# Two-level down product in three more chunks, and weight sums made by negation on ScalarE and adding loads from DRAM

## The chip, the cores and the metric

The kernel runs on one core of a Trainium2 chip, in fp32 throughout. The metric is the device time of one execution in microseconds (us); the median of several executions is compared. The engines are TensorE (PE, matmuls; PEld is its weight load), VectorE (DVE), ScalarE (ACT), GpSimd (POOL), and SyncE (SP), which issues most of the DMAs.

## The reference

An attention without softmax is followed by a mixture of four experts, whose results are all summed:

```python
# q, k, v: (batch 8, heads 8, seq 576, head_dim 64)
kv = np.einsum('bhsd,bhse->bhde', k, v)
out = np.einsum('bhsd,bhde->bhse', q, kv)
rms = np.sqrt(np.mean(out * out, axis=-1, keepdims=True) + 1e-06)
attn = out / rms * g_norm
x = attn.transpose(0, 2, 1, 3).reshape(4608, 512)

# domain_probs: (4608, 4), w1: (4, 512, 1024), w2: (4, 1024, 512)
p = domain_probs / (domain_probs.sum(-1, keepdims=True) + 1e-09)
out = np.zeros((4608, 512))
for e in range(4):
    h = np.maximum(x @ w1[e], 0.0)
    out += p[:, e:e + 1] * (h @ w2[e])
```

## The kernel before

The 4608 tokens are worked on in nine chunks (`NCH`) of 512. A stage `s = e * NCH + c` is one chunk of one expert: first the product with W1 ("up"), a relu, and the product with W2 ("down"). There are 36 stages. The products use a Strassen-like scheme (Winograd's form): a matrix product of 2x2 blocks is made of seven block products instead of eight, at the price of sums of blocks ahead of it and after it. "Two-level" means that each of the seven is again made of seven.

The kernel first records all operations with a sort key (in stages), the engines that may run each one, and the buffers it reads and writes. `Plan.layout` then puts them in a fixed order for each engine, by the keys, an estimate of each operation's cost and the free buffers. The order, and which of VectorE and GpSimd gets a sum, come from there. An adding DMA is issued by GpSimd:

```python
                    else:
                        op.end = busy[eng] = t + op.cost[eng]
                        if op.kb:
                            op.end += 5.5
```

The weights of an expert are loaded as four blocks of 128x1024 for W1 and four for W2; four more blocks of each are sums of them (`form`), made on VectorE or GpSimd. The second level ("inner") then makes four 128x256 sums for each of seven blocks:

```python
    def weights_1(e, key, step, need):
        f = {n: Buf("big", f"w1_{e}_{n}") for n in (1, 2, 21, 4, 5, 6, 7, 3)}
        ...  # loads of 1, 2, 21 and 4 at key + i * step
        def sums():
            form(need + 0.25, 5, 21, 4, ALU.add)
            form(need + 0.26, 6, 5, 1, ALU.subtract)
            form(need + 0.5, 7, 1, 21, ALU.subtract)
            form(need + 0.5, 3, 2, 6, ALU.subtract)
            ...  # inner sums, at need + j / 7
    def weights_2(e, key, step, deep):
        f = {n: Buf("big", f"w2_{e}_{n}") for n in (1, 12, 2, 3, 5, 6, 7, 4)}
        ...  # loads of 1, 2, 12 and 3
        def form(k_, o, a, b, op):
            combine(
                k_, either(1024), lambda: f[o].ap[:], lambda: f[a].ap[:], lambda: f[b].ap[:], op,
                [f[a], f[b]], [f[o]],
            )
        form(key + 4 * step, 5, 12, 1, ALU.subtract)
        form(key + 5 * step, 6, 3, 5, ALU.subtract)
        form(key + 6 * step, 7, 3, 12, ALU.subtract)
        form(key + 7 * step, 4, 2, 6, ALU.subtract)
        w2f[e] = f
        def inner():
            ...  # 28 inner sums of 128x256 into seven buffers "w2y", at deep + j / 7
```

"w2y" are buffers that the attention used before (their old names `kv`, `kvbd`, `x_rem` stand in the profile). `combine` records a sum that either VectorE or GpSimd may run; such sums are marked `port`, and the scheduler plans no two of them at a time.

The up product is two-level in every stage but the first. The down product has two versions. `down` is one-level, with 14 products of four matmuls with 256 columns, each merged into the output rows:

```python
    def down(s, e, c):
        ...
        for t in range(2):
            for j, m in enumerate(MERGED):          # seven products
                def product(eng, m=m, t=t, ps=ps):
                    for kt in range(4):
                        nc.tensor.matmul(
                            ps.ap[:, 0:HN], lhsT=four(h[m])[:, kt // 2, t, kt % 2, :],
                            rhs=w2f[e][m].ap[:, kt * HN:(kt + 1) * HN],  # L1095
                            ...
                merge(key - 0.4, [ps], ..., i, half, fresh)  # 8 of 14 on ACT, 6 on DVE
```

`down_deep` is two-level: for each of seven outer products it makes forms of the hidden values (one sum of 512 columns and two of 256, `combine`), runs seven inner products of two matmuls with 128 columns, takes them out of PSUM on ScalarE (`copy`) and VectorE (`total`), and sums the seven results to four output blocks:

```python
    def down_deep(s, e, c):
        ...
        for i, group in enumerate(((1, 6), (7, 5), (4, 2), (3,))):
            ...  # forms of the hidden values
            for j, mm in enumerate(ORDER):          # seven inner products
                def product(eng, group=group, mm=mm, ps=ps, forms=forms):
                    for o, m in enumerate(group):
                        b, at = forms[m][mm]
                        for kt in range(2):
                            nc.tensor.matmul(       # L1170
                                ps.ap[:, o * P:(o + 1) * P], lhsT=b.ap[:, col:col + P],
                                rhs=w2q[e][m][mm][1]()[:, kt, :], ...)
```

The stages are recorded in this loop. Expert 0 and each expert's last chunk use `down`; the other 24 stages use `down_deep`:

```python
    weights_2(0, 0.25, 0.02, 0.0)
    ...
    for e in range(E):
        for c in range(NCH):
            s = e * NCH + c
            if e + 1 < E and c == NCH - 1:
                weights_1(e + 1, s + 0.0, 0.12, s + 0.3)()
                inner[e + 1] = weights_2(e + 1, s + 0.6, 0.1, s + 1.3)
            ...
            if s:
                up(s, e, x_views.pop(s))
            if c == 0 and e:
                inner[e]()
            if e and c < NCH - 1:
                ...
                down_deep(s, e, c)
            else:
                down(s, e, c)
```

Every fp32 matmul of the code stands as two records in the profile.

Of the kernel before, what the change touches and what calls it, by code (L numbers as in the profile page):

```python
# [34 lines left out]
class Plan:  # L35
# [45 lines left out]
    def layout(self, slots, later, idle, idle_banks, idle_until):  # L81
# [51 lines left out]
        while left:  # L133
# [4 lines left out]
            for eng in todo:  # L138
                if busy[eng] > t:
                    continue  # L140
                pending = todo[eng]
                while pending and pending[0].start is not None:
                    pending.pop(0)
                if not pending:
                    continue
                reach = pending[0].key + self.REACH[eng]
                best = None
                for op in pending:
                    if op.key > reach:
# [12 lines left out]
                    if eng in ("PE", "SP"):  # L162
                        break
                if best is not None:
                    op = best
                    op.start, op.eng = t, eng
                    if eng == "SP":
                        busy[eng] = t + op.cost[eng]
                        bus = max(bus, t + 1.5) + op.kb / 215.0
                        op.end = bus + 0.5  # L170
                        lanes = lanes[1:] + [op.end]
                    else:
                        op.end = busy[eng] = t + op.cost[eng]
                        if op.kb:
                            op.end += 5.5
                    if op.port:
                        port = op.end
                        heapq.heappush(wake, port)
                    for b in op.outs:
                        if b.kind is not None and b.slot is None:  # L180
                            free[b.kind].sort()
                            b.slot = free[b.kind].pop(0)[1]
                            b.ap = slots[b.kind][b.slot]
                    for b in op.bufs:
                        b.left -= 1
                        if b.left == 0 and b.kind is not None:
                            end = max(o.end for o in [op] + b.readers + b.writers) + self.CROSS
                            free[b.kind].append((end, b.slot))
                            live[b.kind] -= 1
                            ended[b.kind] = max(end, ended.get(b.kind, 0.0))  # L190
                            for rule in [r for r in later if not any(live.get(k) for k in r[0])]:
                                later.remove(rule)
                                end = max(ended[k] for k in rule[0])
                                for ap in rule[2]:
                                    free.setdefault(rule[1], []).append((end, len(slots[rule[1]])))
                                    slots[rule[1]].append(ap)
                                heapq.heappush(wake, end)
                    heapq.heappush(wake, busy[eng])
                    heapq.heappush(wake, op.end + self.SAME)
                    heapq.heappush(wake, op.end + self.CROSS)  # L200
                    order.append(op)
                    left -= 1
                    moved = True
                if eng == "PE" and busy[eng] <= t and 1.6 <= t and front < idle_until:
                    kind, spare = next((
                        (k, f) for k in idle_banks for f in free[k] if f[0] <= t
                    ), (None, None))
                    if spare is not None:
                        op = Op(front, {"PE": 0.23}, None, (), (), 0, False)
                        op.start, op.eng, op.end = t, eng, t + 0.23  # L210
                        op.fn = lambda eng, bank=slots[kind][spare[1]]: idle(bank)
                        busy[eng] = op.end
                        free[kind].remove(spare)
                        free[kind].append((op.end, spare[1]))
                        heapq.heappush(wake, op.end)
                        order.append(op)
                        moved = True
# [13 lines left out]
def kernel(  # L231
# [181 lines left out]
    def w2_src(e, uh, dh):  # L413
        rows = moe_w2[e][uh * HF:(uh + 1) * HF, dh * HN:(dh + 1) * HN]
        return rows.rearrange("(kt p) d -> p kt d", p=P)

    def weights_1(e, key, step, need):

        f = {n: Buf("big", f"w1_{e}_{n}") for n in (1, 2, 21, 4, 5, 6, 7, 3)}
        corner = {}  # L420
        w1corner[e] = {}
        for i, (n, dh, uh) in enumerate(((1, 0, 0), (2, 1, 0), (21, 0, 1), (4, 1, 1))):
            corner[n] = Buf(None, f"w1c_{e}_{n}")
            w1corner[e][uh, dh] = f[n], corner[n]
            load(
                key + i * step, f[n],
                lambda n=n: f[n].ap[:].rearrange("p (k u) -> p k u", k=2),
                w1_src(e, dh, uh), 512, also=[corner[n]],
            )

        def form(k_, o, a, b, op):
            corner[o] = Buf(None, f"w1c_{e}_{o}")
            combine(
                k_, either(1024), lambda: f[o].ap[:], lambda: f[a].ap[:], lambda: f[b].ap[:], op,
                [f[a], f[b], corner[a], corner[b]], [f[o], corner[o]],
            )

        def sums():
            form(need + 0.25, 5, 21, 4, ALU.add)
            form(need + 0.26, 6, 5, 1, ALU.subtract)  # L440
            form(need + 0.5, 7, 1, 21, ALU.subtract)
            form(need + 0.5, 3, 2, 6, ALU.subtract)
            w1f[e] = {}
            for j, m in enumerate(OUTER):
                x, low, y = f[m], corner[m], Buf("w1y", f"w1y_{e}_{m}")
                parts = {}
                for n, (uq, kt) in ((1, (0, 0)), (2, (0, 1)), (7, (1, 0)), (4, (1, 1))):
                    parts[n] = (
                        [x, low] if n == 7 else [x],
                        lambda x=x, uq=uq, kt=kt: two(x.ap[:])[:, kt, uq * HN:(uq + 1) * HN],  # L450
                    )
                for n, at in ((5, 0), (6, 1), (3, 2)):
                    parts[n] = ([y], lambda y=y, at=at: y.ap[:, at * HN:(at + 1) * HN])
                for o, a, b, op in (
                    (5, 7, 4, ALU.add), (7, 1, 7, ALU.subtract), (6, 5, 1, ALU.subtract),
                    (3, 2, 6, ALU.subtract),
                ):
                    combine(
                        need + j / 7, either(HN), parts[o][1], parts[a][1], parts[b][1], op,
                        parts[a][0] + parts[b][0], [low] if o == 7 else [y],  # L460
                    )
                w1f[e][m] = parts

        return sums

    def weights_2(e, key, step, deep):
# [12 lines left out]
                [f[a], f[b]], [f[o]],  # L479
            )  # L480

        form(key + 4 * step, 5, 12, 1, ALU.subtract)
        form(key + 5 * step, 6, 3, 5, ALU.subtract)
        form(key + 6 * step, 7, 3, 12, ALU.subtract)
        form(key + 7 * step, 4, 2, 6, ALU.subtract)
        w2f[e] = f

        def inner():
# [792 lines left out]
    sums_1()  # L1281
    x_forms(0, 0.3)
    x_views = {}
    weights_2(0, 0.25, 0.02, 0.0)
    norm_probs(0.3)
    inner = {}
    for e in range(E):
        for c in range(NCH):
            s = e * NCH + c
            if e == 0 and c + 1 < B:  # L1290
                attention(c + 1, s - 0.1, 0.8, s + 0.5)
            if e + 1 < E and c == NCH - 1:
                weights_1(e + 1, s + 0.0, 0.12, s + 0.3)()
                inner[e + 1] = weights_2(e + 1, s + 0.6, 0.1, s + 1.3)
            if s + 1 < E * NCH:
                if e == 0 and c + 1 < NCH:
                    x_views[s + 1] = x_forms(c + 1, s + 0.7)
# [1 line left out]
                    x_views[s + 1] = x_again((c + 1) % NCH, s + (0.05 if e else 0.6), 0.13)  # L1299
            if s:  # L1300
                up(s, e, x_views.pop(s))
            if c == 0 and e:
                inner[e]()
            if e and c < NCH - 1:
                if not primed:
                    banks = [Buf("ab", f"prime{i}") for i in range(2)]

# [66 lines left out]
```

## Time and profile before

| | before |
|---|---|
| time, median of 3 runs | 1729.79 us (1729.73 to 1730.35) |
| span of the profiled execution | 1728.2 us |
| instructions | 38444 |
| granted TensorE clock | 1.000 |
| DMA | 220.94 MB, 128 GB/s on average |

The busy line of the page gives each engine's busy time, its share of the span, and its number of instructions. A line of waits gives the engine and what it was about to do, after the arrow who released it, and then the total in us, the number of times and the longest. A line of a stretch gives the busy time of each engine in it, with the number of instructions in brackets, then the granted clock, the busy share of the DMA engines and GB/s. A line of the chain of work gives start and duration in us, then the engine, what it wrote, the line of the program, and how many instructions in a row. A group of instructions is given with its line, engine, operation, what it writes and reads, shapes and count; then busy us and mean ns of one; then the engine's idle time ahead of them and what ended it. A DMA line gives the count, the size of one transfer, and the median us from its issue to its landing. L360 is the line of all sums recorded by `combine`, L881 the up product, L908 and L900 its ways out of PSUM, L1236 the sums of output blocks.

### The profile page before, as it was taken

The page shows a single profiled execution, that of the slowest core. Times are in us where ns is not written, and L with a number is a line of the kernel's source. Part 1 is how long each engine was busy: PE and PEld are TensorE (multiplying, and loading weights), DVE is VectorE, ACT ScalarE, POOL GpSimd, SP SyncE. Part 2 cuts the span into 40 slices and gives each one's busy share as a digit, 9 for nine tenths or more (in the row PEclk, how much of TensorE's full clock was granted, in tenths as well). Part 3 has the DMA queues.
Part 4 walks back from the last instruction along what each step waited for, and adds up shares of the span by engine and source line. Part 5 has one row for each costly group of instructions (what it writes and reads, how often), then busy time and mean ns, then how long its engine had stood idle before and what let it go on. Part 6 is the DMA issues. An engine that isn't in the chain of part 4 may idle for free.

```text
span 1728.2 us, 38444 instructions
## 1 busy us (share of the span) xinstructions
PE 1718.7 (99%) x15334; PEld 1651.4 (96%) x15334; DVE 1224.7 (71%) x1969; ACT 939.3 (54%) x2300; POOL 614.8 (36%) x560
## 2 busy tenths in 40 slices
PE   9999999999999999999999999999999999999998
PEld 7699999999999999999999999999999999999998
DVE  4755655565676777777788877777788877777774
ACT  3454544554444565656555556566655566565652
POOL 2421323133334333333345333333345433333331
PEclk9999999999999999999999999999999999999999
DMA  9756444633433353444464344444475344444442
GB/s 236 224 159 193 154 120 131 193 135 128 147 129 100 93 115 103 115 107 113 131 186 110 99 110 111 111 111 110 109 208 112 98 111 111 111 111 103 114 102 49
DMA packets 148596, 220.94 MB, mean 128 GB/s; under 512 B 49600, under 2 KB 90816, under 8 KB 148416
## 3 DMA queue, kind: packets, MB, share of 16 engines
q1 hardware_dynamic: 133312, 191.21, 35.5%
q0 software_dynamic: 15104, 27.27, 10.8%
q8 instruction: 120, 1.97, 0.5%
q14 instruction: 60, 0.49, 0.1%
HBM read 145.30 MB, written 73.14 MB: 126 GB/s over the span
## 4 chain that ended last, share of the span: by engine, by line
PE 99%; POOL 1%; DVE 0%; ACT 0%; issue 0%; POOLq 0%
PE u L881 45%; PE db L1170 19%; PE db L1095 14%; PE ab L1170 12%; PE ab L1095 2%; PE u L968 2%; PE ab L634 1%; PE ab L1323 1%; PE ab L620 1%; PE ab L678 1%; PE ab L660 1%; PE u L1095 1%; POOL rt L551 0%; PE db L660 0%; PE ab L722 0%; PE ab L704 0%
## 5 line engine op out<-in xcount | busy, mean ns | idle before, releaser
L360 DVE TENSOR_TENSOR big<-big,big 128x1024 f32<-128x1024 f32 (+1 forms) x450 | 442.5, 997 | 36.0 <-ACT big L864 23.8
L881 PE MATMUL u<-xf,big 128*128 128x128 f32 x3104 | 453.0, 275 | 0.0
L881 PEld LDWEIGHTS u<-xf,big 128*128 128x128 f32 x3104 | 401.3, 192 | 2.2
L881 PE MATMUL u<-xf,w1y 128*128 128x128 f32 x2652 | 389.6, 275 | 0.0
L908 DVE TENSOR_TENSOR big<-u,snap 128x256 f32<-128x256 f32 x430 | 181.5, 422 | 235.1 <-PE u L881 175.7
L881 PEld LDWEIGHTS u<-xf,w1y 128*128 128x128 f32 x2652 | 343.4, 192 | 2.2
L900 ACT ACTIVATE snap<-u 128x256 f32<-128x256 f32 x490 | 188.1, 384 | 251.3 <-PE u L881 213.9
L1095 PE MATMUL db<-big,big 128*128 128x256 f32 x1120 | 264.1, 380 | 2.1 <-DVE big L560 2.1
L1095 PEld LDWEIGHTS db<-big,big 128*128 128x128 f32 x1120 | 202.9, 190 | 24.6 <-DVE big L560 2.3
L900 ACT ACTIVATE big<-u 128x256 f32<-128x256 f32 x430 | 165.0, 384 | 110.4 <-PE u L881 74.3
L360 POOL TENSOR_TENSOR big<-big,big 128x256 f32<-128x256 f32 (+1 forms) x138 | 170.2, 1241 | 131.6 <-DVE big L360 44.1
L1170 PE MATMUL db<-big,big 128*128 128x128 f32 x1056 | 146.7, 275 | 0.0
L864 ACT ACTIVATE big<-big 128x1024 f32<-128x1024 f32 x128 | 134.4, 1050 | 2.6 <-POOL big L360 1.3
L1170 PEld LDWEIGHTS db<-big,big 128*128 128x128 f32 x1056 | 132.1, 192 | 0.1
L1236 POOL TENSOR_TENSOR big<-big 128x512 f32<-128x512 f32 x26 | 32.9, 1266 | 269.2 <-DVE big L360 263.9
L1198 ACT ACTIVATE snap<-db 128x256 f32<-128x256 f32 x192 | 68.5, 357 | 99.8 <-PE db L1170 94.9
L360 POOL TENSOR_TENSOR big<-big 128x512 f32<-128x512 f32 (+1 forms) x57 | 70.7, 1240 | 126.9 <-DVE big L360 102.6
L1170 PE MATMUL db<-kv,big 128*128 128x128 f32 x804 | 114.6, 275 | 0.0
L1065 POOL DMA_DIRECT2D out_dram<-big x100 | 91.1, 987 | 48.2 <-ACT snap L1198 22.8
L900 ACT ACTIVATE u<-u 128x256 f32<-128x256 f32 x245 | 90.9, 371 | 27.9 <-PE u L881 8.0
L1170 PEld LDWEIGHTS db<-kv,big 128*128 128x128 f32 x804 | 102.1, 192 | 0.1
L1206 DVE TENSOR_TENSOR big<-ab,snap 128x256 f32<-128x256 f32 x140 | 59.2, 423 | 56.7 <-ACT snap L1198 31.9
(218 smaller groups left out, 2686.3 us busy)
## 6 DMA issues: line engine op xcount, KB each, us to landing
xf<-x SPq DMA_DIRECT2D x108, 512.0 KB, 3.6
out_dram<-big POOLq DMA_DIRECT2D x84, 256.0 KB, 5.7
xf<-x_h SPq DMA_DIRECT2D x81, 256.0 KB, 3.0
xf<-x SPq DMA_DIRECT2D x81, 256.0 KB, 3.2
x<-xf SPq DMA_DIRECT2D x36, 512.0 KB, 6.7
big<-in_moe_w_dram SPq DMA_DIRECT2D x25, 512.0 KB, 4.9
small<-in_q_dram SPq DMA_DIRECT2D x72, 128.0 KB, 4.8
kv<-in_k_dram SPq DMA_DIRECT2D x30, 288.0 KB, 5.0
```

Of the source, the lines that this page charges most:

```text
L360: lambda eng: adder(eng).tensor_tensor(out=out_(), in0=a(), in1=b(), op=op),
L864: lambda eng: nc.scalar.activation(out=b.ap[:], in_=b.ap[:], func=ACT.Relu),
L881: nc.tensor.matmul(ps.ap[:, u * P:(u + 1) * P], lhsT=w1f[e][m][mm][1]()[:, u * P:(u + 1) * P], rhs=views[m][mm][1](), start=(mm in (1, 5) ...
L900: lambda eng: nc.scalar.activation(out=where(), in_=ps.ap[:, 0:HN], func=ACT.Copy),
L908: lambda eng: nc.vector.tensor_tensor(out=block(whole, a, t), in0=src.ap[:, 0:HN], in1=add_.ap[:], op=ALU.add),
L968: nc.tensor.matmul(bank.ap[:], lhsT=two(w.ap[:])[:, kt, ut * P:(ut + 1) * P], rhs=two(xh[dh].ap[:])[:, kt, :], start=(dh == kt == 0), stop ...
L1065: nc.gpsimd.dma_start(out=dst, in_=cell(i)[parts, :], accum_op=ALU.add)
L1095: nc.tensor.matmul(ps.ap[:, 0:HN], lhsT=four(h[m])[:, kt // 2, t, kt % 2, :], rhs=w2f[e][m].ap[:, kt * HN:(kt + 1) * HN], start=(m in (1, ...
L1170: nc.tensor.matmul(ps.ap[:, o * P:(o + 1) * P], lhsT=b.ap[:, col:col + P], rhs=w2q[e][m][mm][1]()[:, kt, :], start=(mm in (1, 5) and o == ...
L1198: lambda eng: nc.scalar.activation(out=where(), in_=group_of(ps.ap), func=ACT.Copy),
L1206: lambda eng: nc.vector.tensor_tensor(out=cell(tq, dq), in0=group_of(src.ap), in1=group_of(add_.ap), op=ALU.add,),
L1236: lambda eng: adder(eng).tensor_tensor(out=whole(to), in0=whole(a), in1=whole(b), op=ALU.add),
```

## The change

Three things are changed. First, the last chunk of the first three experts (stages 8, 17 and 26) uses the two-level down product; only the very last stage still uses the one-level one. Expert 0 gets the inner sums of its W2 for that, placed at stage 7.6 and after. Second, of the eight 128x1024 sums that each of the experts 1 to 3 needs for its weights, six are made in another way: `subtract_from` writes -a on ScalarE, and a DMA from DRAM adds the other operand, which is a block of the weights as it was given, into the same buffer. This takes the sum off VectorE and GpSimd, which only issues the DMA. Third, the keys at which the next expert's weights are loaded and summed are moved, and the scheduler counts 9.0 us for such a load to land.

```diff
                         if op.kb:
-                            op.end += 5.5
+                            op.end += 9.0 if op.kb == 512 else 5.5
 ...
+    def subtract_from(key, to, view, a, src, reads, writes):
+        plan.add(
+            key, act(2 * NT),
+            lambda eng: nc.scalar.activation(
+                out=to.ap[:], in_=a.ap[:], func=ACT.Copy, scale=-1.0),
+            reads=reads, writes=[to],
+        )
+        plan.add(
+            key, {"POOL": 1.0},
+            lambda eng: nc.gpsimd.dma_start(out=view(to.ap), in_=src, accum_op=ALU.add),
+            reads=[to], writes=writes, kb=512,
+        )
 ...
             form(need + 0.26, 6, 5, 1, ALU.subtract)
-            form(need + 0.5, 7, 1, 21, ALU.subtract)
-            form(need + 0.5, 3, 2, 6, ALU.subtract)
+            if e:
+                from_dram(need + 0.5, 7, 21, 0, 0)
+                from_dram(need + 0.5, 3, 6, 1, 0)
+            else:
+                form(need + 0.5, 7, 1, 21, ALU.subtract)
+                form(need + 0.5, 3, 2, 6, ALU.subtract)
 ...
-        form(key + 4 * step, 5, 12, 1, ALU.subtract)
-        form(key + 5 * step, 6, 3, 5, ALU.subtract)
-        form(key + 6 * step, 7, 3, 12, ALU.subtract)
-        form(key + 7 * step, 4, 2, 6, ALU.subtract)
+        for i, o, b, uh, dh, a in (
+            (4, 5, 12, 0, 1, 1), (5, 6, 3, 1, 1, 5), (6, 7, 3, 1, 1, 12), (7, 4, 2, 1, 0, 6)
+        ):
+            if e:
+                subtract_from(
+                    key + i * step, f[o], lambda ap: ap[:].rearrange("p (k d) -> p k d", k=4),
+                    f[a], w2_src(e, uh, dh), [f[a]], [f[o]],
+                )
+            else:
+                form(key + i * step, o, b, a, ALU.subtract)
 ...
-    weights_2(0, 0.25, 0.02, 0.0)
+    inner = {0: weights_2(0, 0.25, 0.02, 7.6)}
 ...
-                weights_1(e + 1, s + 0.0, 0.12, s + 0.3)()
-                inner[e + 1] = weights_2(e + 1, s + 0.6, 0.1, s + 1.3)
+                weights_1(e + 1, s + 0.0, 0.12, s + 0.4)()
+                inner[e + 1] = weights_2(e + 1, s + 1.0, 0.13, s + 1.55)
 ...
-            if c == 0 and e:
+            if s == NCH - 1 or c == 0 and e:
                 inner[e]()
-            if e and c < NCH - 1:
+            if NCH - 1 <= s < E * NCH - 1:
```

More of the change, by code (lines that the diff above doesn't have):

```diff
@@ L436, in form, with from_dram @@
             )
+        def from_dram(k_, o, a, dh, uh):
+            corner[o] = Buf(None, f"w1c_{e}_{o}")
+            subtract_from(
+                k_, f[o], lambda ap: ap[:].rearrange("p (k u) -> p k u", k=2), f[a],
+                w1_src(e, dh, uh), [f[a], corner[a]], [f[o], corner[o]],
+            )
         def sums():
@@ L480, in form @@
             )
-        form(key + 4 * step, 5, 12, 1, ALU.subtract)
-        form(key + 5 * step, 6, 3, 5, ALU.subtract)
-        form(key + 6 * step, 7, 3, 12, ALU.subtract)
-        form(key + 7 * step, 4, 2, 6, ALU.subtract)
+        for i, o, b, uh, dh, a in (
+            (4, 5, 12, 0, 1, 1), (5, 6, 3, 1, 1, 5), (6, 7, 3, 1, 1, 12), (7, 4, 2, 1, 0, 6)
+        ):
+            if e:
+                subtract_from(
+                    key + i * step, f[o], lambda ap: ap[:].rearrange("p (k d) -> p k d", k=4),
+                    f[a], w2_src(e, uh, dh), [f[a]], [f[o]],
+                )
+            else:
+                form(key + i * step, o, b, a, ALU.subtract)
         w2f[e] = f
@@ L1283 @@
     x_views = {}
-    weights_2(0, 0.25, 0.02, 0.0)
+    inner = {0: weights_2(0, 0.25, 0.02, 7.6)}
     norm_probs(0.3)
-    inner = {}
     for e in range(E):
```

## The prediction

> **What bounds the kernel now.** I read the busy times of the page first, then the waits of TensorE, then the busy times in stretches of 48 us, and last the groups of instructions by form.
>
> ```profile
> PE 1718.7 (99%) x15334; PEld 1651.4 (96%) x15334; DVE 1224.7 (71%) x1969; ACT 939.3 (54%) x2300; POOL 614.8 (36%) x560
> ```
>
> TensorE (PE) is busy for all but 9.5 us of 1728.2. A busy TensorE could still hide slow issue, so next come the waits of PE, all of them:
>
> ```profile
> PE db L1095 <- DVE big L560: 2.1, 1, 2.1
> PE ab L1323 <- POOL ident masks.py:199: 1.4, 1, 1.4
> PE u L881 <- ACT snap L900: 0.6, 1, 0.6
> PE u L881 <- ACT u L900: 0.5, 1, 0.5
> PE ab L678 <- ACT big L686: 0.4, 1, 0.4
> ```
>
> Five waits, 5.0 us. The stretches say where: only the first 96 us have PE below full. From there on it is without a gap:
>
> ```profile
> core 0: us, PE busy (x) PEld busy (x) DVE busy (x) ACT busy (x) POOL busy (x), PEclk, DMA share, GB/s
> 672.00:720.00 48.00, 48.00 (x432) 48.00 (x432) 36.48 (x57) 28.74 (x72) 14.97 (x14) 1.00 0.43 111
> ...
> 864.00:912.00 48.00, 48.00 (x425) 47.79 (x424) 39.83 (x62) 27.86 (x74) 25.28 (x23) 1.00 0.61 171
> 912.00:960.00 48.00, 48.00 (x336) 45.31 (x335) 41.36 (x64) 24.80 (x58) 26.78 (x30) 1.00 0.55 126
> 960.00:1008.00 48.00, 48.00 (x433) 48.00 (x431) 39.64 (x61) 28.07 (x72) 17.36 (x17) 1.00 0.36 93
> ```
>
> So the time is the number of matmuls times the pitch at which they are issued, and each microsecond of matmul taken out is a microsecond of the kernel, if the others keep up. The second thing to see is who might not: in the change of experts (864 to 960) VectorE (DVE) is busy 39.83 + 41.36 = 81.2 of 96 us, 85%, against 76% in the steady stretch at 672.
>
> **What the Trainium skill says.** *Perfetto Trace Analysis*, "Identifying the Most-Contended Engine", warns that matmul busy time is no measure of closeness to the peak and asks for the LDWEIGHTS share. The trace agrees: the matmul records last 275 ns each, but 432 of them fit in 48 us. I therefore count by pitch, not by duration. PEld is 48.00 of 48 where all matmuls are 128 wide.
>
> *DMA: Bandwidth & Descriptors*, "Rules for kernel authors", has transfers that accumulate issued from GpSimd, as here. In "Anatomy of one DMA — SWDGE (gpsimd) path" it fits 2.0 us + bytes/436e3 per transfer, which would be 2.6 us for 256 KB. The trace disagrees, its adding stores take more than twice that, and the measurement decides:
>
> ```profile
> out_dram<-big POOLq DMA_DIRECT2D x84, 256.0 KB, 5.7
> ...
> out_dram<-big POOLq DMA_DIRECT2D x16, 128.0 KB, 4.6
> ```
>
> *SBUF — State Buffer*, "SBUF: two separate sides", says that a VectorE operation with two SBUF inputs and a GpSimd operation that reads SBUF exclude each other for a whole instruction. The trace fits: VectorE's 128x1024 sums into "small" take 1212 ns at the least and 2185 at the most. The kernel's scheduler knows of it: sums marked `port` on either engine are planned one after the other, and GpSimd's wait for VectorE's. VectorE's don't wait for GpSimd's, so on the chip they can still run into one another, which lengthens the row.
>
> **The change part by part.** (1) Last chunks. The stages s = 8, 17 and 26 (last chunk of experts 0, 1, 2) change from the plain down product to the two-level one. Plain: 14 products of 4 matmuls, each in two passes, 112 records of 256 columns. Two-level: 98 matmuls, 196 records of 128 columns. The pitches come from the chain of work and the stretches:
>
> ```profile
> 923.96 5.18 PE db L1095 x24
> 930.03 3.46 PE db L1095 x16
> ```
>
> 5.18/24 = 0.216 us for 256 columns; 48.00/432 = 0.1111 us for 128 columns. Plain costs 112 x 0.216 = 24.2 us, two-level 196 x 0.1111 = 21.8 us. That saves 2.4 us a stage and 7.2 us in three. Counted in the built kernels, matmuls of 256 columns go from 672 to 504 and of 128 from 5782 to 6076, which is 3 x 56 less and 3 x 98 more. Nothing else changes on TensorE.
>
> (2) What the two-level product adds elsewhere. Each converted chunk needs seven sets of forms of the hidden values (one 512 and two 256 wide each), more evictions, and seven sums of output blocks; expert 0 also needs its 28 inner sums of W2 (256 wide), which it did not have. Plain merges on VectorE fall away.
>
> (3) What the negations take off. Experts 1 to 3 each lose six 1024-wide subtractions on VectorE or GpSimd, 18 in all (VectorE 356 to 342, GpSimd 65 to 61), and get a 1024-wide negation on ScalarE and an adding load of 512 KB issued by GpSimd for each.
>
> The sum by engine, counts from the built orders and durations from these rows and their like:
>
> ```profile
> L360 DVE TENSOR_TENSOR big<-big,big 128x1024 f32<-128x1024 f32 x264 | 350.3, 1331 | 34.9 <-ACT big L864 23.8 <-PE db L1170 1.7 <-PE u L881 0.8
> L864 ACT ACTIVATE big<-big 128x1024 f32<-128x1024 f32 x128 | 134.4, 1050 | 2.6 <-POOL big L360 1.3 <-DVE big L360 1.2
> L360 DVE TENSOR_TENSOR big<-big,big 128x256 f32<-128x256 f32 x186 | 95.2, 523 | 1.1 <-POOL big L360 0.4
> L360 POOL TENSOR_TENSOR big<-big 128x512 f32<-128x512 f32 x52 | 66.6, 1281 | 124.1 <-DVE big L360 101.4 <-DVE big L1236 12.3 <-DVE small L360 3.2
> ```
>
> VectorE: -14 x 1.33, +57 x 0.52 (256 wide), +10 x 0.9 (512 wide), +6 x 0.29, -18 x 0.48 (merges), +18 x 0.42 and +6 x 0.29 (sums out of PSUM) = +22 us. GpSimd: -4 x 2.36, +32 x 1.27, +13 x 0.74, -6 x 0.46, and 18 issues at about 1.3 us (0.94 us for 128 rows, 0.84 for 64, so an estimate for 256 to 512 rows) = +62 us. ScalarE: 18 x 1.05 + 45 x 0.38 + 15 x 0.28 = +40 us. All three lie beside TensorE. Per transition that is +7, +21 and +13 us, spread over some 150 us.
>
> So the change of words is misleading: VectorE is not relieved. The negations pay for part of what the deeper product costs it.
>
> (4) Do the adding loads come in time? From 128 to 256 KB a landing gets 1.1 us longer, so I estimate 5.7 + 2.2 = 7.9 us for 512 KB, and 9 with the negation ahead of it. In the built order I looked for the last matmul that must end before each adding load and the first that needs it: between them stand 15.8 to 49 us of matmuls at the pitches above. Three W2 sums hang on one another (5, 6, 4), some 27 us, and the order gives this chain room too. I expect no wait here.
>
> (5) Does VectorE keep up? I laid its instructions out in built order at these mean durations, none ahead of the matmul it depends on, and compared each end with the start of the matmul that needs it. Before, the smallest margin after 96 us is +0.2 us, and the trace indeed has no wait. After, the first transition keeps +0.3 us or more, but in the second and third one the margin falls to -1.0 us (around 960 and 1350 us), at evictions of the up product behind inner sums of W1. With the longer means that the old transition shows (1.42 us for 1024 wide) it falls to about -2. I put this at 1.0 to 2 us of TensorE waiting in each of the two, 3 us together.
>
> Sum: 1729.8 - 7.2 + 3.0 = 1725.6 us.
>
> **Rivals.** *All of the 7.2 us arrives.* For it: TensorE had no wait in three transitions at 85% VectorE, and a margin of -1 us is within the error of my durations. Against: VectorE gets no lighter, and GpSimd, which excludes it, gets 21 us more. It makes 1722.5.
>
> *VectorE becomes the bound in the transitions.* For it: 11.4 of 12 us busy in the worst stretch of the old transition (884 to 896), more GpSimd sums to share the SBUF port with. Against: inner sums have been moved later (W2's key from s + 1.3 to s + 1.55), so the load is spread. With 3 to 4 us lost in each of the three it makes 1731 to 1735; in two of them, 1728 to 1731.
>
> *Adding loads land late.* W2's rows are 1 KB, twice as many pieces as a store of the same size, and beside them run loads and stores at a DMA share of 0.6. Landings of adding stores ran from 3.0 to 8.7 us. If 512 KB took 13 us, ScalarE would stand at a negation with evictions behind it, and TensorE would wait some 2 us each, 4 to 10 us in all: 1726 to 1733.
>
> **Range and chances.** The saving on TensorE is sure to some 0.3 us; the loss is between 0 and 8. I give 1725.6 us, and 1722.5 to 1730.0 for 8 in 10. Neither 2% (34.6 us) is in reach: the whole gain is 0.4%, and a loss of 40 us would need TensorE to stand at every transition for 14. Chances: faster by over 2% 0.01, within 2% 0.97, slower by over 2% 0.02.
>
> **What would show it.** 504 matmuls of 256 columns and a TensorE busy time near 1711.5 us confirm step 1. New waits of PE on VectorE (or on ScalarE behind it), 2 to 4 us, near 960 and 1350 us and none near 540 confirm step 5. Landings of the adding loads near 8 us, with ScalarE not waiting long at its second and third negations, confirm step 4. The prediction is wrong if the busy time falls by less than 6 us, or if PE waits for more than 6 us after 96 us.

## The result, and the profile after

| | before | after |
|---|---|---|
| time, median of 4 runs | 1729.88 us (1729.73 to 1730.35) | 1723.16 us (1722.72 to 1723.45) |
| ratio to before | | 0.996, 95% interval 0.9943 to 0.9978 |
| span of the profiled execution | 1728.2 us | 1720.9 us |
| DMA moved | 220.94 MB | 230.42 MB |

The change takes 6.7 us off, and the spans differ by 7.3 us. The busy line of after:

```profile
PE 1711.4 (99%) x15586; PEld 1653.1 (96%) x15586; DVE 1233.4 (72%) x2034; ACT 975.1 (57%) x2378; POOL 677.4 (39%) x613
```

TensorE (PE) is busy 7.3 us less than before, with 252 records more: three stages went from 112 records of 256 columns to 196 of 128, and 3 x 84 = 252. The other three engines all have more to do: VectorE 8.7 us, ScalarE 35.8 us, GpSimd 62.6 us. The waits of PE in after, all of them:

```profile
PE db L1126 <- DVE big L591: 2.1, 1, 2.1
PE ab L1353 <- POOL ident masks.py:199: 1.4, 1, 1.4
PE u L912 <- ACT snap L931: 0.6, 1, 0.6
PE u L912 <- ACT u L931: 0.5, 1, 0.5
PE ab L709 <- ACT big L717: 0.4, 1, 0.4
```

These are the five waits of before, to the tenth, under line numbers that have moved by 30 or 31 (L881 is now L912, L900 L931, L908 L939, L1095 L1126, L1170 L1201, L1198 L1229, L1206 L1237, L1236 L1267). All lie in the first 96 us. The stretches of after, where the prediction looked:

```profile
core 0: us, PE busy (x) PEld busy (x) DVE busy (x) ACT busy (x) POOL busy (x), PEclk, DMA share, GB/s
672.00:720.00 48.00, 48.00 (x432) 48.00 (x431) 38.06 (x54) 30.14 (x76) 21.07 (x17) 1.00 0.44 107
864.00:912.00 48.00, 48.00 (x433) 48.00 (x431) 39.77 (x68) 30.78 (x76) 25.67 (x26) 1.00 0.75 187
912.00:960.00 48.00, 48.00 (x432) 48.00 (x431) 40.98 (x72) 31.61 (x77) 24.66 (x26) 1.00 0.66 152
960.00:1008.00 48.00, 48.00 (x432) 48.00 (x431) 34.43 (x62) 30.32 (x77) 29.07 (x27) 1.00 0.47 118
```

In the change of experts there are 432 or 433 matmuls to 48 us, as many as in the steady stretch at 672. In before 912 to 960 held 336, because the stage in it was made of 256-column products. VectorE is no busier there than it was (40.98 against 41.36). The adding loads, in the view of their line (durations of the issue on GpSimd in ns, minimum/median/maximum; then the landing):

```profile
L427 POOL DMA_DIRECT2D big<-in_moe_w_dram x16: 1211/1297/1870, 495.9 to 1329.4; - x16
L427 POOL DMA_DIRECT2D small<-in_moe_w_dram x2: 1341/1490/1639, 497.0 to 923.4; - x2
...
DMA to landing us min/median/max: 5.7/7.2/9.4
```

Eighteen loads, landed after 7.2 us in the median and 9.4 us at most, and no matmul waits for any of them.

### The profile page after: what moved, and what is told of

Its sections match the earlier page's. It is cut to its first block, busy times and chain, and to the rows that moved or that the text cites. A ratio compares the mean times of both kernels' runs of the same rounds, so it can differ in the third digit from the quotient of the medians.

```text
span 1720.9 us, 39248 instructions
## 1 busy us (share of the span) xinstructions
PE 1711.4 (99%) x15586; PEld 1653.1 (96%) x15586; DVE 1233.4 (72%) x2034; ACT 975.1 (57%) x2378; POOL 677.4 (39%) x613
## 2 busy tenths in 40 slices
DMA packets 156567, 230.42 MB, mean 134 GB/s; under 512 B 49888, under 2 KB 97248, under 8 KB 156384
## 3 DMA queue, kind: packets, MB, share of 16 engines
q1 hardware_dynamic: 133312, 191.21, 35.8%
## 4 chain that ended last, share of the span: by engine, by line
PE 99%; POOL 1%; DVE 0%; ACT 0%; issue 0%; POOLq 0%
PE u L912 45%; PE db L1201 21%; PE ab L1201 13%; PE db L1126 12%; PE u L999 2%; PE ab L665 1%; PE ab L1353 1%; PE ab L651 1%; PE ab L709 1%; PE ab L691 1%; PE u L1126 1%; PE ab L1126 0%; POOL rt L582 0%; PE db L691 0%; PE ab L753 0%; PE ab L735 0%
## 5 line engine op out<-in xcount | busy, mean ns | idle before, releaser
L912 PE MATMUL u<-xf,big 128*128 128x128 f32 x3104 | 452.4, 275 | 0.0
L912 PEld LDWEIGHTS u<-xf,big 128*128 128x128 f32 x3104 | 399.8, 192 | 1.4
L912 PE MATMUL u<-xf,w1y 128*128 128x128 f32 x2652 | 390.9, 275 | 0.0
L939 DVE TENSOR_TENSOR big<-u,snap 128x256 f32<-128x256 f32 x442 | 186.4, 422 | 232.8 <-PE u L912 162.2
L912 PEld LDWEIGHTS u<-xf,w1y 128*128 128x128 f32 x2652 | 343.2, 192 | 1.6
L931 ACT ACTIVATE snap<-u 128x256 f32<-128x256 f32 x490 | 188.2, 384 | 207.2 <-PE u L912 175.2
L931 ACT ACTIVATE big<-u 128x256 f32<-128x256 f32 x442 | 169.5, 384 | 119.8 <-PE u L912 93.2
L360 POOL TENSOR_TENSOR big<-big,big 128x256 f32<-128x256 f32 (+1 forms) x137 | 180.4, 1321 | 126.5 <-DVE big L360 61.4
L1126 PE MATMUL db<-big,big 128*128 128x256 f32 x904 | 213.8, 379 | 2.1 <-DVE big L591 2.1
L1126 PEld LDWEIGHTS db<-big,big 128*128 128x128 f32 x904 | 163.3, 190 | 19.9 <-DVE big L591 2.3
L1201 PE MATMUL db<-big,big 128*128 128x128 f32 x1204 | 166.8, 275 | 0.0
L1201 PEld LDWEIGHTS db<-big,big 128*128 128x128 f32 x1204 | 150.4, 192 | 0.1
L895 ACT ACTIVATE big<-big 128x1024 f32<-128x1024 f32 x128 | 134.7, 1052 | 4.5 <-DVE big L360 3.8
L1229 ACT ACTIVATE snap<-db 128x256 f32<-128x256 f32 x216 | 77.0, 356 | 105.8 <-PE db L1201 102.7
L1201 PE MATMUL ab<-kv,big 128*128 128x128 f32 x764 | 110.1, 275 | 0.0
L931 ACT ACTIVATE u<-u 128x256 f32<-128x256 f32 x245 | 91.0, 371 | 32.3 <-PE u L912 12.4
L1201 PE MATMUL db<-kv,big 128*128 128x128 f32 x752 | 109.1, 275 | 0.0
L1267 POOL TENSOR_TENSOR big<-big 128x512 f32<-128x512 f32 x25 | 31.7, 1269 | 177.6 <-DVE big L360 144.4
L578 POOL TENSOR_SCALAR ss<-ss 128x16 f32<-128x16 f32 (+2 forms) x26 | 6.4, 245 | 240.7 <-DVE ss L571 240.4
```

Of the source, the lines that this page charges most:

```text
L360: lambda eng: adder(eng).tensor_tensor(out=out_(), in0=a(), in1=b(), op=op),
L895: lambda eng: nc.scalar.activation(out=b.ap[:], in_=b.ap[:], func=ACT.Relu),
L912: nc.tensor.matmul(ps.ap[:, u * P:(u + 1) * P], lhsT=w1f[e][m][mm][1]()[:, u * P:(u + 1) * P], rhs=views[m][mm][1](), start=(mm in (1, 5) ...
L931: lambda eng: nc.scalar.activation(out=where(), in_=ps.ap[:, 0:HN], func=ACT.Copy),
L939: lambda eng: nc.vector.tensor_tensor(out=block(whole, a, t), in0=src.ap[:, 0:HN], in1=add_.ap[:], op=ALU.add),
L1126: nc.tensor.matmul(ps.ap[:, 0:HN], lhsT=four(h[m])[:, kt // 2, t, kt % 2, :], rhs=w2f[e][m].ap[:, kt * HN:(kt + 1) * HN], start=(m in (1, ...
```

## The experiments

All edits below are to the kernel after, unless said otherwise. Medians of the kernel before beside the three groups of runs were 1730.41, 1730.39 and 1730.47 us, half a microsecond above the pair of the table, so ratios carry the comparison across groups. Where a kernel issues 15586 matmul records as after does, I also compared the start of the n-th record in the two traces: where the difference grows, time is lost. "Lost" below is that growth within one change of experts. In the three runs with repeated sums TensorE's order is that of after, record by record. Where a sum changes its engine or an estimate changes, the plan is laid out anew and TensorE's order changes with it: in the runs without negations, with W1's or W2's alone, and with the other estimate, 26% to 36% of the matmuls write another tile than the one at the same place of after. There "lost" gives a size, and the rebuilt order is one more thing that differs. The moved keys stay in all experiments, so what they are worth was not measured.

**Two-level stages without the negations.** Is the gain the stages alone, as the prediction's sum has it, or do the negations carry it? All eight weight sums of every expert are made on VectorE or GpSimd again; the stages and the keys stay.

```diff
-            if e:
+            if False:
                 from_dram(need + 0.5, 7, 21, 0, 0)
 ...
-            if e:
+            if False:
                 subtract_from(
```

> The changed kernel (two-level product in all three last chunks, new keys) with all eight weight sums of each expert kept on VectorE or GpSimd, no negation and no adding load. Theory A (the matmuls alone make the time; VectorE and GpSimd have room for 18 more sums of 1.2 to 2.4 us): as the changed kernel, 1723 us, no wait of TensorE after 96 us. Rival B (the negations are what makes room; without them VectorE and the sums become late at the changes of experts): TensorE waits at the transitions, 3 us or more in each, 1732 us or more.

It took 1736.17 us (1735.89 to 1736.68), ratio 1.0033 (1.002 to 1.0046): slower than before, with the same matmuls as after. The weight loads of TensorE (PEld) now wait between 440 and 1500 us:

```profile
PEld u L912 <- ACT u L931: 4.3, 10, 0.9
PEld u L912 <- ACT snap L931: 2.6, 10, 0.5
PEld u L912 <- DVE small L939: 0.8, 1, 0.8
PEld ab L1201 <- ACT ab L1229: 0.7, 1, 0.7
PEld db L1201 <- ACT snap L1229: 0.5, 1, 0.5
PEld db L1201 <- DVE big L1237: 0.3, 1, 0.3
PEld db L1201 <- ACT big L1229: 0.2, 1, 0.2
PEld u L912 <- DVE big L939: 0.2, 1, 0.2
```

The longest of these waits is 0.9 us; they are many and short. After has none in the same window. The engine that ends them is mostly ScalarE: 8.3 us of this list, against 1.3 us for VectorE. Two of them, in the timelines of ScalarE and of TensorE (in brackets the idle time before, and who ended it):

```profile
507.90 0.37 ACT L931 ACTIVATE u<-u 128x256 f32<-128x256 f32 x1 [2.30 <-PE u L912]
508.32 0.71 PE L912 MATMUL u<-xf,w1y 128*128 128x128 f32 x4 [0.52 <-ACT u L931]
...
1351.28 1.05 ACT L895 ACTIVATE small<-small 128x1024 f32<-128x1024 f32 x1
1352.23 0.38 ACT L931 ACTIVATE u<-u 128x256 f32<-128x256 f32 x1
1352.66 0.71 PE L912 MATMUL u<-xf,w1y 128*128 128x128 f32 x4 [0.74 <-ACT u L931]
```

In the first, ScalarE has stood idle for 2.30 us until the matmuls end that it takes out; the matmul that needs the result comes so soon in TensorE's order that it must wait. In the second, ScalarE is still at a relu of 1024 columns (L895) when the way out is due. In neither does the wait end on VectorE.

VectorE's load has changed too. Counted in the built orders, 17 of the 18 sums that come back go to GpSimd (1024-wide sums there 61 to 78) and one to VectorE (342 to 343). The stretches of this kernel:

```profile
core 0: us, PE busy (x) PEld busy (x) DVE busy (x) ACT busy (x) POOL busy (x), PEclk, DMA share, GB/s
912.00:960.00 48.00, 47.99 (x428) 47.65 (x427) 34.57 (x66) 28.61 (x74) 25.23 (x21) 1.00 0.53 132
960.00:1008.00 48.00, 47.78 (x411) 46.31 (x410) 43.28 (x79) 27.88 (x72) 23.13 (x22) 1.00 0.40 101
```

After had 40.98 and then 34.43 us of VectorE in these two stretches; here it is 34.57 and then 43.28. VectorE's work is put off and comes in a heap, and in the stretch of the heap only 411 matmuls get through. The trace says which work: between 960 and 1008 VectorE runs 32 sums of 256 columns on the line of `combine` instead of 21, and 12 of 1024 instead of 9. GpSimd, with the wide sums on its hands, runs fewer of the small ones: 67 of 256 columns instead of 89, counted over the ten stretches of 48 us around the three changes (496 to 640, 864 to 1056, 1296 to 1440). A plan in which VectorE's sums come late may leave TensorE few products that are ready, so that dependent ones stand close together; that would join the heap to the waits on ScalarE, but no run tests it.

**The negations without the stages.** Last chunks one-level again, as before.

```diff
-            if s == NCH - 1 or c == 0 and e:
+            if c == 0 and e:
                 inner[e]()
-            if NCH - 1 <= s < E * NCH - 1:
+            if e and c < NCH - 1:
```

> The changed kernel with its negations, adding loads and new keys, but the one-level product in the last chunks as before. Theory A (time is matmuls times pitch): 1729.8 us as before, within 0.5, no wait of TensorE after 96 us. Rival C (taking 1024-wide sums off VectorE and GpSimd is worth time by itself): below 1728 us.

1731.75 us (1731.12 to 1733.24), ratio 1.0009 (1.0 to 1.0017). By themselves the negations bring nothing; the kernel is 1.3 us slower than before, where theory A allowed 0.5. One wait of TensorE is new, at a merge of a one-level chunk at 1324 us, and is about as long as that:

```profile
PE db L1126 <- DVE big L1080: 1.4, 1, 1.4
```

**One stage.** As in the last run, but stage 17 is two-level: `if e and (c < NCH - 1 or s == 2 * NCH - 1):`.

> The changed kernel with the two-level product in the last chunk of expert 1 alone (stage 17); the last chunks of experts 0 and 2 stay one-level. Theory A: a third of the saving, 112 x 0.216 - 196 x 0.1111 = 2.4 us, so 1727.4 us and a span of 1725.8 us in the profile. Rival D (the stages are not alike; part of the gain comes from elsewhere): off by more than 1 us.

1728.61 us (1727.88 to 1730.03), ratio 0.999 (0.9984 to 0.9997). That is 1.8 us under before and 3.1 under the negations alone, against a stage's 2.4. It is 1.2 us above the 1727.4 of theory A, 0.7 with the half microsecond of the groups. There are 15418 records, 84 more than before, and TensorE is busy 1717.0 us. Three stages from 1731.75 to the 1723.16 of after, or 1723.7 with the half microsecond of the groups, make 2.7 us each, a little more than 2.4. That fits the wait of 1.4 us going too, which neither the kernel with one stage nor after has. So the unit of step 1 holds within half a microsecond a stage, and it adds up.

**How much more can VectorE bear?** The inner sums of W1 of experts 1 to 3 that VectorE runs (all but one of each four) are repeated; the repeats only write the same values again.

```diff
+                    made.times = 4 if e and o != 7 else 1
 ...
-            made = op.fn(op.eng)
+            for _ in range(op.times if op.eng == "DVE" else 1):
+                made = op.fn(op.eng)
```

> The changed kernel with three of the four inner sums of W1 (those that don't work in place) of experts 1 to 3 done four times where VectorE has them: some 16 sums per expert, so 48 more per expert. Theory E (VectorE's sums of 256 columns follow each other at 0.335 us, and evictions have about 1.2 us to spare): 48 x 0.335 = 16 us more per transition, of which idle time takes some 6 to 10; TensorE waits 3 to 10 us per transition, 1732 to 1750 us. Rival F (the durations of 0.51 us of the prediction hold, and its margin of -1 us is real): 48 x 0.51 = 24 us more, 15 us or more of waiting per transition, over 1765 us.

One run: 1778.31 us. 138 sums of some 0.43 us, about 60 us of VectorE, cost 55 us (lost 10.3, 22.0 and 22.3). Theory E's range missed, and the number of rival F came: with this dose VectorE's extra work comes through. F's reason, that there is no room at all, falls with the next run. Almost all of the waits of TensorE's weight loads end on VectorE's way out of PSUM (line numbers are one to two higher in these kernels):

```profile
PEld u L914 <- DVE big L941: 36.1, 20, 4.2
```

A part of the 55 is a slower clock, told of under the next dose but one: the trace has 27.3 us at half clock in the three changes, which is worth up to 13.7 us. With each sum twice instead of four times:

> The changed kernel with three of the four inner sums of W1 of experts 1 to 3 done twice where VectorE has them, 46 more sums in all against 138 in the run before, at the same places of the same order. In that run a repeated sum took 0.43 us. Theory E (in the changed kernel VectorE has about 1.2 us to spare at each eviction, and the idle time between takes up the rest): 46 x 0.43 = 20 us more work, of which TensorE waits for less than half: 1724 to 1732 us. Rival F (the margin of -1 us is real, so that the transitions have no room at all): all of it comes through, 1742 us or more.

One run: 1729.49 us. Of 46 added sums, about 20 us, 5.7 us come through (lost 0.3, 2.7 and 2.7 in the three changes), in short waits again; TensorE's weight loads waited so:

```profile
PEld u L914 <- DVE big L941: 4.7, 10, 0.7
```

**Is it the busy share or the burst?** In stages 13, 22 and 31, far from the changes of experts, the 256-wide forms of the hidden values are made three times: 60 added sums, 26 us.

```diff
+                    made.times = 3 if s in (13, 22, 31) else 1
```

> The changed kernel with the 256-wide forms of the hidden values done three times where VectorE has them, in one steady stage of each of experts 1 to 3 (stages 13, 22 and 31): 60 more sums of 0.43 us, 26 us, 9 us in each of the three. Theory E (steady stages have the room that transitions lack: VectorE is busy 36.5 of 48 us): less than 6 us come through in all, 1723 to 1729 us. Rival (VectorE's order is as tight everywhere, its idle time cannot be used): 15 us or more, 1738 us or more.

One run: 1739.14 us. I had expected the steady stages to swallow it, as VectorE is busy only 79% there (38.06 of 48 us), and that fell; the rival's 1738 us or more came. Each of the three stages lost 5.2 us, after one wait:

```profile
PEld u L913 <- DVE big L940: 9.5, 3, 3.2
```

The forms stand close together in the order, ahead of one way out of PSUM, and the way out comes late once. The stretches around the first, each 3.4 us long:

```profile
core 0: us, PE busy (x) PEld busy (x) DVE busy (x) ACT busy (x) POOL busy (x), PEclk, DMA share, GB/s
742.00:745.40 3.40, 3.39 (x31) 3.20 (x30) 3.30 (x7) 2.51 (x6) 0.00 (x0) 1.00 1.01 195
745.40:748.80 3.40, 0.47 (x5) 0.28 (x3) 3.23 (x10) 0.38 (x1) 0.18 (x1) 1.00 0.04 7
748.80:752.20 3.40, 3.34 (x17) 3.34 (x18) 1.40 (x5) 0.00 (x0) 3.00 (x3) 0.57 0.28 73
```

TensorE stands for about 3 us, and then works for 3.4 us at a clock of 0.57, with 17 matmuls where it had 31. The wait itself is 3.2 us; the slow clock after it makes it 5.2. What counted for VectorE here, then, was the length of a burst ahead of one way out of PSUM, not the average.

**The scheduler's estimate of a landing.** 5.5 us for all transfers, instead of 9.0 for the adding loads: `op.end += 5.5`.

> The changed kernel with the scheduler counting 5.5 us in place of 9.0 for an adding load to land (7.2 us is the median in the changed kernel's profile). Only the order differs. Theory H (the loads lie under 15 us or more of matmuls, the estimate does not matter): 1723 us within 1. Rival G (operations are placed ahead of data that lands later, and the engines wait in their order): TensorE waits 1 to 3 us at each transition, 1726 to 1732 us.

1725.13 us (1724.81 to 1725.62), ratio 0.9969 (0.9958 to 0.9981). Lost 0.2, 0.7 and 0.9 us, in waits of 0.3 us at most on the ways out of PSUM. The loads land after 7.2 us in the median, so a plan with 5.5 us takes them as done before they are; that this makes the waits was not traced, and TensorE's order differs as well. It is a matter of 1 to 2 us, between the two theories.

**W1's or W2's negations?** Only W1's two sums by negation (W2's condition `if False:`), and only W2's four.

> The changed kernel with negation and adding load for the two W1 sums of each of experts 1 to 3 only; the four W2 sums stay on VectorE or GpSimd. All eight sums there cost 13 us in the run with no negation (4.4 us at each change of experts). Theory L (each 1024-wide sum taken off makes the same room): 6 of 18 sums are off, so 13 x 12/18 = 8.7 us remain, 1732 us. Rival M (the W1 sums alone are what is late, being needed first): 1723 to 1726 us.

> The changed kernel with negation and adding load for the four W2 sums of each of experts 1 to 3 only; the two W1 sums stay on VectorE or GpSimd. Theory L: 12 of 18 sums are off, 13 x 6/18 = 4.4 us remain, 1727.5 us. Rival M (the W1 sums alone are what is late): nearly all of the 13 us remain, 1732 to 1736 us. Rival N (the last sums to stay find enough room): 1723 to 1725 us.

1730.29 us (1729.69 to 1730.63), ratio 1.0 (0.9991 to 1.0008), and 1729.14 us (1728.49 to 1730.04), ratio 0.9992 (0.9984 to 1.0001). Without W2's negations 6.6 us are lost, without W1's 5.7, without both 13.3: they add up roughly, and neither kind is the one that matters. Division by the number of sums missed by 1.6 to 1.7 us in both runs: it gave W2's twelve more than they have, and W1's six less. As without any negation, most of the waits end on ScalarE (3.5 us against 1.4 for VectorE with W1's alone, 3.7 against 0.6 with W2's alone). W1's are worth most in the first change (3.1 us are lost there without them), W2's in the second and third (3.1 in each).

**The very last stage two-level too.** `if NCH - 1 <= s:`, which takes another 2.4 us of matmuls off.

> The changed kernel with the two-level product in the very last stage too. Theory A: 2.4 us less of matmuls, 1720.8 us, less what the end gets longer. Rival K (after the last matmul the two-level product has sums of blocks and two merges to go before the last store, 2 to 4 us more than the one-level one): 1722.5 to 1725 us.

1726.87 us (1726.21 to 1727.15), ratio 0.9979 (0.9971 to 0.9988), worse than after and above the rival's range too. At the end nothing hides the sums. The chain of work that ended last, in this kernel (start us, us, what):

```profile
1713.85 0.91 PE ab L1201 x8
...
1714.78 0.44 DVE big L1237
...
1715.31 1.29 DVE big L1267 x2
...
1719.53 0.48 DVE big L1080
```

The last matmuls end at 1714.76, and 5.3 us of sums and merges (L1080) come after them. After ends its matmuls at 1716.37 and has one merge of 0.48 us to do:

```profile
1714.63 1.74 PE u L1126 x8
...
1716.40 0.48 DVE big L1080
```

The one-level product is the right one for the last stage.

**Expert 0's sums by negation as well.** W2's alone (its condition `if True:`), and then W1's also.

> The changed kernel with negation and adding loads for the W2 sums of expert 0 too, which are made in the first 70 us, where TensorE still waits for some 5 us. Theory O (these sums stand ahead of the scaling of the attention on VectorE and GpSimd, for which TensorE waits 2.1 us near 74 us): 1 to 2 us less, 1721 to 1722 us. Rival P (the DMA engines are at 0.97 in the first 48 us, the adding loads land late and the first down product waits): 1724 us or more. Without effect: 1723 us.

> As the run before, with two of the four W1 sums of expert 0 made by negation and adding load as well, so that six of eight are in all four experts. Theory O: 1721 to 1722 us, a little better than the run before. Rival P: W1's sums are needed from the second stage on, the loads land late, TensorE waits there; 1724 us or more.

1723.06 us (1721.74 to 1723.4), ratio 0.9954 (0.9941 to 0.9968): the same as after within the intervals, which overlap. In its profile the wait near 73 us, which the change aimed at, is 1.4 us instead of 2.3 for the weight loads, but a stretch at half clock follows it, told of in the last section. Two of its five executions were granted a clock of 1.000 and span 1720.0 and 1720.1 us, against 1720.9 for the two such of after: a gain of 0.8 us may be there, on too few executions to say. With W1's also 1728.6 us (1726.8 to 1729.99), ratio 0.9989 (0.9983 to 0.9996). At 72 us of that one products with W1 are held up, and 6.8 us at half clock follow:

```profile
PEld u L912 <- issue: 4.0, 1, 4.0
```

The profile shows no releaser for this wait. That the way over DRAM is too long for a place where no stage of matmuls lies ahead of it fits, but was not tested. No kernel here is clearly faster than after.

## Why the prediction was right, and where not

The time was put at 1725.6 us and came out at 1723.16, inside the range and 2.4 us below the number given. It is the wait of 3.0 us in the sum that did not come, less half a microsecond of the 7.2. The rival "All of the 7.2 us arrives", at 1722.5, is what happened.

*Step 1, last chunks.* Right. -7.2 us was the sum, TensorE's busy time fell by 7.3, to 1711.4 where 1711.5 was named, and the run with one stage fits the unit of 2.4 us.

*Steps 2 and 3, the sum by engine.* Of +22, +62 and +40 us, GpSimd (+62.6) and ScalarE (+35.8) were right. VectorE got only +8.7 by the page. Its instructions are 65 more, as counted; their records add up to 17.1 us more (1315.4 to 1332.5), and the busy line counts only once the time in which two records overlap. Of the rest, 5.4 us are shorter records of the sums of output blocks (0.79 us in the mean at 512 columns, where before had 0.84).

*"The negations pay for part of what the deeper product costs it."* Too little. Without them the same stages are 13 us slower than after. With the keys as they are, they are worth nothing alone and are the condition of the gain. The prediction weighed them by busy time. What differs without them is more: 17 wide sums on GpSimd, a heap of sums on VectorE in the change of experts, another order of TensorE, and waits that end on ScalarE for 8.3 us and on VectorE for 1.3. The 13 us are shown; which of these makes them stays open.

*Step 4, the loads.* Right. 7.2 us from issue to landing where 7.9 was estimated, 1.3 us an issue as estimated, no wait.

*Step 5, "Does VectorE keep up?"* This step failed: it took 3 us for waits that did not come. The durations were too long. TensorE's matmuls were counted by pitch, because a record of 275 ns stands for 111 ns of progress; VectorE's sums were counted by mean duration of their records. They overlap too. The timeline of VectorE in after, in the change of experts (start us, us, then what it is):

```profile
915.00 0.41 DVE L360 TENSOR_TENSOR w1y<-w1y,big 128x256 f32<-128x256 f32 x1
915.34 0.41 DVE L360 TENSOR_TENSOR big<-big,big 128x256 f32<-128x256 f32 x1
915.67 0.41 DVE L360 TENSOR_TENSOR big<-big 128x256 f32<-128x256 f32 x1
916.00 0.41 DVE L360 TENSOR_TENSOR big<-big,big 128x256 f32<-128x256 f32 x1
916.34 0.41 DVE L360 TENSOR_TENSOR w1y<-big,w1y 128x256 f32<-128x256 f32 x1
```

Records of 0.41 us start every 0.335 us. The prediction took 0.51 for this shape. The Trainium skill, *Vector Engine (DVE) Microarchitecture Reference*, "5.2 Measured stream behaviour on trn2 (trn3 not measured)", has the rate: 1.0417 ns per column and about 75 ns per instruction "after queue overlap", measured there on integer streams, which makes an estimate of 342, 608 and 1142 ns at 256, 512 and 1024 columns. The trace agrees: after 440 us the medians from start to start, where one sum follows the last at once, are 335, 602 and 1142 ns, while the medians of the records are 416, 681 and 1224. The means, which hold the sums that were blocked, are 0.44, 0.77 and 1.30 us from start to start, and 0.54, 0.92 and 1.36 by record. The step used means by record.

I then laid VectorE's instructions out once more, in the same way but at mean pitches (0.42 us for 256 columns, 0.80 for 512, 1.28 for 1024, 0.34 for 256 out of PSUM; between the means of the two traces), for after and for seven of the experiments. This is hindsight, but the runs judge it. The smallest margin by the layout, in us, and the time lost, for the first / second / third change of experts:

```
kernel                     margin by durations    margin by pitches     lost
after                       0.3 / -1.0 / -1.0      0.8 /  0.6 /  0.8     0   / 0    / 0
no negations               -3.0 / -7.6 / -5.9     -1.5 / -4.4 / -3.0     5.4 / 3.5  / 4.4
only W1's                   0.4 / -2.7 / -2.7      0.8 / -1.3 / -1.3     0.3 / 3.1  / 3.1
only W2's                  -2.8 / -2.6 / -2.6     -1.9 / -0.3 / -0.3     3.1 / 1.3  / 1.3
landing estimate 5.5        0.1 / -0.2 / -0.2      0.8 /  0.4 /  0.4     0.2 / 0.7  / 0.9
inner sums twice           -2.6 / -6.1 / -6.1      0.1 / -2.4 / -2.4     0.3 / 2.7  / 2.7
inner sums four times     -10.7 /-22.6 /-22.6     -5.1 /-11.5 /-11.5    10.3 / 22.0 / 22.3
forms three times (13, 22, 31)   -5.1 each              -2.9 each        5.2 each
```

At pitches a margin of 0.6 or more lost at most 0.3 us, one of 0.1 to 0.4 at most 0.9, and a negative one lost 1.3 to 22 us. These bounds were drawn after the fact, and no further kernel tried them. At durations after is put at -1.0, and it lost nothing. Measured in the trace of after, the shortest time from the end of one of VectorE's ways out of PSUM in these changes to the start of the matmul that needs it is 0.47 us; for ScalarE's it is 0.26 us.

The layout holds VectorE's order alone, with TensorE on time. In the three runs with repeated sums, where nothing else was changed, the waits do end on VectorE (all of the 42.8 and 4.9 us with the inner sums, 9.5 of 10.1 us with the forms), so there its lateness is shown as the cause. In the runs with a rebuilt order a low margin goes with a loss, but most of the waits end on ScalarE, so that VectorE makes them late is not shown. Nor does the layout give the size: without negations the first change loses 5.4 us at a margin of -1.5. Whether the SBUF port that GpSimd's wide sums share with VectorE adds to it was not separated, and the one new wait of the negations alone (1.4 us at a merge) doesn't show in it.

*The rivals.* "VectorE becomes the bound in the transitions" did not happen here; it is what the repeated inner sums bring about. Without the negations the changes of experts lose as much as this rival named (3.5 to 5.4 us each), but with waits that end mostly on ScalarE. "Adding loads land late" fell.

## What to carry to other kernels

Where one engine is without a gap, a change is worth the time it takes off that engine only if the others' bursts still fit; lay out each engine's own order by the pitch of its instructions, start to start, and not by the length of their records, and then read in the trace which engine ends the waits. A part of a change that brings nothing by itself can be what makes another part pay, so undo each part alone before calling it idle. At the very end of this kernel nothing hides side work, and there the plain form wins.

## What the runs showed of the hardware

A short stop of TensorE can cost more than its length. In the run with forms made three times the trace grants half the clock for 3.4 us after each of the three waits of 3.2 us, and each costs 5.2 us: 3.2 + 3.4/2 = 4.9. The Trainium skill, *TensorE: Matmul & The Clock Gate*, "Part 1: The HAM clock gate", lets TensorE fall to half clock after an idle window of about 3.4 us, and come back after a busy one; the length agrees. The waits here are a little shorter than that window. None of 0.9 us or less, as in the kernel without negations, was followed by a slow stretch. A dip stands at about 73 to 76 us in ten of the twelve experiments and not in before, after, the kernel without negations and the one with W2's alone. It comes right after a wait of the weight loads that is 2.3 us long in nearly all kernels, before and after included: the same wait is followed by a slow stretch in one execution and not in another. Nine of the ten dips are 3.4 us long, and those kernels are 0.5 to 1.0 us behind by 82 us, so I put that lag down to the dip and not to the edits, which was not tested; with expert 0's W1 also by negation the wait is 4.0 us, the dip 6.8 us and the lag 4.1 us.
